# A semaphore wait that makes GpSimd follow VectorE's step at their common port

## The chip, the core and the metric

The kernel runs on one core of a Trainium2 chip. A core has five engines that run side by side, each with its own queue that it works through in order: TensorE (matmuls, PE in the profile), VectorE (DVE), ScalarE (ACT), GpSimd (POOL) and SyncE (SP, which issues most of the DMAs here). Between engines order comes from semaphores alone: an instruction waits until a counter has reached a value. The metric is device time in microseconds of one execution. Before the change it was 2434.4 us, the median of three runs (2433.55 to 2434.43).

## The reference, cut to what matters

Channel attention is followed by a feed-forward layer with a rational function between its two products.

```
qn, kn = q and k, divided by their norms over the 6080 tokens     # 4 batches, 256 channels
a = softmax(kn^T @ qn / tau)                                      # 256 x 256 for each batch
x = (v @ a), all tokens in one list                               # 24320 x 256
h = x @ w_in                                                      # 24320 x 2048
g = (a0 + a1 h + a2 h^2 + a3 h^3) / (1 + |b0||h| + |b1| h^2 + 1e-6)
out = g @ w_out                                                   # 24320 x 256
```

## The kernel before, in words

The softmax and w_in are multiplied once for each batch ("fused" weights, tile `w`), so that the long part is: values times fused weights, rational function, times w_out. Every fp32 factor is split into a high and a low part, and three products stand for one (`vhi`/`vlo`, `w` in two tiles, `gh`/`gl`, `w_high`/`w_low`).

The tokens go in groups of 512 (48 groups, 12 for each batch), and the 2048 hidden channels in 8 pairs of 128. One pair of one group, called a pair step below, is 128 x 1024 elements and passes these engines (function `pair`):

- TensorE: 12 matmuls into one of three PSUM buffers `hx`.
- ScalarE: `d` (twice: size, then square), `uu` (slope), `r` (inverse root, then its square).
- VectorE: "num" `hx<-uu,fit,hx`; "high" `gh<-hx,fit,r`; "back" `d<-d,gh`; "rest" `d<-hx,fit,d`. Rest is the last reader of `hx`, and TensorE may fill that buffer again when it is done.
- GpSimd: "low" `gl<-d,r`.
- TensorE: 8 matmuls of `gh` and 4 of `gl` into `acc`. At a group's end VectorE turns `acc` into `orow`, which is stored.

Once for each group VectorE also turns the loaded values (`cv<-vst`), ScalarE makes `vhi` of them and GpSimd the rest `vlo<-cv,vhi`. While the groups of one batch run, the q and k rows of the next batch pass through: TensorE multiplies them (`hx<-kq`), VectorE sums that into `sacc`, ScalarE squares them (`sq<-kq`, two buffers) and GpSimd sums the squares (`ssq<-sq,ssq`).

What order the instructions stand in is decided in Python before anything is built. `Planner.add` takes steps with an engine, a cost, a due time (tables `LAG` and `TIME`) and the buffers they read and write. `Planner.order` plays the steps through with these costs: on each engine the ready step with the earliest due time starts. Steps marked `port` (all GpSimd steps, back on VectorE, the transposes of values and some others on VectorE) are taken to need a port that VectorE and GpSimd share: `fits` starts such a step only when the planned port step of the other engine is over. The list that comes out has all steps in order of planned start. It fixes the order on each engine, and `InOrder` keeps it. Between engines the plan's order is not kept: an instruction waits for the data and buffers that it needs, and for nothing else. So a GpSimd step that the plan put behind a back of VectorE may start ahead of it on the chip.

The arm that runs for these inputs is `halves[True]`; it holds 515 GpSimd tensor_tensor steps: 383 `gl`, 48 `vlo` and 84 sums of squares. The last pair step is done by halves (`halved`), with its `gl` on VectorE.

Of the kernel before, what the change touches and what calls it, by code (L numbers as in the profile page):

```python
# [88 lines left out]
class InOrder:  # L89


    def __init__(self, tc, engine):
        self.tc, self.engine = tc, engine

    def __getattr__(self, name):
        op = getattr(self.engine, name)

        def issue(*args, **kwargs):
            ins = op(*args, **kwargs)  # L99
            self.tc.keep_in_program_order(ins)  # L100
            return ins

        return issue
# [14 lines left out]


class Step:  # L120
    __slots__ = ("eng", "cost", "fn", "key", "need", "after", "new", "bufs", "banks", "port", "n")


class Planner:
# [54 lines left out]
    def order(self):  # L179
# [10 lines left out]
        events, out, now = sorted((t, 2, n, None) for n, t in enumerate(busy.values())), [], 0.0  # L190
        port = {"DVE": 0.0, "POOL": 0.0}
# [18 lines left out]
        while left:  # L210
# [34 lines left out]
            while events and events[0][0] <= now:  # L245
                _, what, _, s = heapq.heappop(events)
# [7 lines left out]
                if what == 1:  # L254
                    for b in s.bufs:
                        b.left -= 1
                        if not b.left:
                            free[b.tag].append(b.slot)
        self.trace = out
        return [s for _, s in out]  # L260


@with_exitstack
def tile_channel_attention_rational_ffn(
# [58 lines left out]
    dve = InOrder(tc, nc.vector)  # L323
    act = InOrder(tc, nc.scalar)
    pool = InOrder(tc, nc.gpsimd)
# [89 lines left out]
    def near_root(x):  # L415
        act.activation(near, x, AF.Abs_reciprocal_sqrt)
# [8 lines left out]
    def fit_grow():  # L425
        dve.reciprocal(inv, b1)
        dve.tensor_tensor(left, b0, b0, op=ALU.mult)
        dve.scalar_tensor_tensor(left, left, -0.25, inv, op0=ALU.mult, op1=ALU.mult)
        dve.tensor_scalar(left, left, ONE, None, op0=ALU.add)
        dve.reciprocal(share, left)  # L430
        dve.tensor_tensor(zero, b1, share, op=ALU.mult)

    def fit_reach():
        root_of(grow, zero)
        dve.reciprocal(inv, grow)
        dve.scalar_tensor_tensor(centre, b0, 0.5, inv, op0=ALU.mult, op1=ALU.mult)
        dve.tensor_tensor(centre, centre, share, op=ALU.mult)
        dve.tensor_scalar(sign, a3, 0.0, None, op0=ALU.is_ge)
        dve.tensor_scalar(sign, sign, 2.0, 1.0, op0=ALU.mult, op1=ALU.subtract)
        dve.tensor_tensor(zero, size[:, 3:4], share, op=ALU.mult)  # L440
        for _ in range(3):
            dve.tensor_tensor(zero, zero, inv, op=ALU.mult)

    def fit_rest():
        root_of(reach, zero)
        dve.tensor_tensor(zero, reach, b1, op=ALU.mult)
        dve.reciprocal(left, zero)
        dve.tensor_tensor(shift, a2, sign, op=ALU.mult)
        dve.scalar_tensor_tensor(shift, shift, 0.5, left, op0=ALU.mult, op1=ALU.mult)
        dve.tensor_tensor(drop, a1, sign, op=ALU.mult)  # L450
        dve.tensor_tensor(drop, drop, share, op=ALU.mult)
        dve.tensor_tensor(drop, drop, inv, op=ALU.mult)
        dve.tensor_tensor(left, shift, shift, op=ALU.mult)
        dve.tensor_tensor(drop, drop, left, op=ALU.subtract)
        dve.tensor_tensor(base_a0, a0, sign, op=ALU.mult)
        dve.tensor_tensor(base_a0, base_a0, share, op=ALU.mult)

    def unscaled():
        dve.memset(fit[:, 0:2], 1.0)
        dve.tensor_copy(base_a0, a0)  # L460

    def arm(fast):
# [574 lines left out]
            finish(G, at + NFP * II + due["finish"], acc)  # L1037
        return plan.order()
    halves = {fast: arm(fast) for fast in (True, False)}
    choice = nc.values_load(plain[0:1, 0:1], min_val=0, max_val=1)  # L1040
    with tc.If(choice > 0) as which:
        fit_grow()
        near_root(zero)
        fit_reach()
        near_root(zero)
        fit_rest()
        dve.reciprocal(rtau, coef[:, 6:7])
        for s in halves[True]:
            s.fn()
    with which.Else():  # L1050
        unscaled()
        dve.reciprocal(rtau, coef[:, 6:7])
        for s in halves[False]:
            s.fn()


# [28 lines left out]
```

## Time and profile before

| what | value |
|---|---|
| median of three runs | 2434.4 us |
| the profiled execution | 2432.47 us, its span 2430.6 us |
| TensorE matmuls | 2366.0 us busy, 97% |
| VectorE | 2180.3 us busy, 90% |
| ScalarE | 2160.2 us busy, 89% |
| GpSimd | 1318.9 us busy, 54% |

The profiler takes one execution. The page gives each engine's busy time, and the chain of work that ended last (here 90% of it TensorE). The trace gives single instructions: start and length in us, engine, source line, operation, tiles written and read, shape, and in brackets the idle time before it with what ended it. All steps are recorded by one helper, so they share line 99 and are told apart by their tiles. The granted clock (PEclk) is TensorE's share of its full speed of 2.4 GHz in a stretch; half of it is the lower level of 1.2 GHz.

### The profile page before, as it was taken

Reading aid. Unit: us, or ns where it says so; the run is one execution under the profiler, and the core shown is the slowest. Engines: PE = TensorE matmul, PEld = TensorE weight load, DVE = VectorE, ACT = ScalarE, POOL = GpSimd, SP = SyncE. Lnnn points to the kernel's source line nnn. Section 1 sums busy time; section 2 is a strip of 40 time slices with the busy share of each in tenths; the row PEclk is TensorE's granted clock in tenths of the full one; section 3 lists DMA queues with packets and bytes.
Section 4 is the critical chain, followed back from the end, with each engine's and each line's share of the span. In section 5 each row is a group of like instructions: output and inputs, shape, how many; then the busy total and the mean of one; then the engine's idle time right before and its main releaser. Section 6 shows DMA issues by size and latency. Waiting matters only on the chain.

```text
span 2430.6 us, 29239 instructions
## 1 busy us (share of the span) xinstructions
PE 2366.0 (97%) x10304; PEld 1945.9 (80%) x10304; DVE 2180.3 (90%) x1959; ACT 2160.2 (89%) x2192; POOL 1318.9 (54%) x522
## 2 busy tenths in 40 slices
PE   7889999999999999999999999999999999999998
PEld 6767788888888788888888878888888788888887
DVE  8888999999977899999997789999998999999997
ACT  4678999999888799999988879999997999999996
POOL 5476555554557655554546855554554445555553
PEclk9999999999999999999999999999999999999999
DMA  9542111111124211111112411111111111111101
GB/s 294 172 114 58 25 19 27 27 26 18 27 52 131 72 22 26 27 27 17 27 27 50 133 31 27 27 24 21 26 27 18 17 27 27 19 26 27 26 9 18
DMA packets 457037, 110.04 MB, mean 45 GB/s; under 512 B 405168, under 2 KB 453808, under 8 KB 456880
## 3 DMA queue, kind: packets, MB, share of 16 engines
q1 hardware_dynamic: 454736, 107.84, 20.7%
q8 instruction: 83, 1.36, 0.2%
q14 instruction: 74, 0.61, 0.1%
q10 hardware_dynamic: 2144, 0.23, 0.1%
HBM read 83.10 MB, written 24.90 MB: 44 GB/s over the span
## 4 chain that ended last, share of the span: by engine, by line
PE 90%; DVE 4%; ACT 2%; DMA 2%; issue 1%; SPq 0%; POOL 0%; ACTq 0%; DVEq 0%; POOLq 0%
PE hx L99 49%; PE acc L99 42%; DVE d L99 2%; DVE hx L99 1%; ACT d L99 1%; DMA kq<-in_q_dram 1%; DMA d<-in_moe_w_in_dram 1%; DVE gh L99 0%; ACT r L99 0%; ACT uu L99 0%; DMA r<-in_k_dram 0%; SPq L99 0%; DVE acc L99 0%; DVE orow L99 0%; DVE fit L99 0%
## 5 line engine op out<-in xcount | busy, mean ns | idle before, releaser
L99 POOL TENSOR_TENSOR gl<-d,r 128x1024 fp32r<-128x1024 f32 (+1 forms) x383 | 955.7, 2501 | 1015.6 <-DVE d L99 660.3
L99 PE MATMUL hx<-vhi,w 128*128 128x512 f32 (+1 forms) x3072 | 901.1, 395 | 16.9 <-DVE d L99 15.2
L99 PEld LDWEIGHTS hx<-vhi,w 128*128 128x128 f32 x3072 | 579.1, 189 | 149.4 <-DVE d L99 10.7
L99 DVE SCALAR_TENSOR_TENSOR gh<-hx,fit,r 128x1024 fp32r<-128x1024 f32 (+1 forms) x385 | 484.8, 1259 | 101.3 <-ACT r L99 93.5
L99 DVE SCALAR_TENSOR_TENSOR d<-d,gh 128x1024 f32<-128x1024 f32 (+1 forms) x385 | 539.8, 1403 | 1.6
L99 DVE SCALAR_TENSOR_TENSOR hx<-uu,fit,hx 128x1024 f32<-128x1024 f32 (+1 forms) x385 | 487.6, 1267 | 57.1 <-ACT uu L99 56.5
L99 ACT ACTIVATE d<-hx 128x1024 f32<-128x1024 f32 (+1 forms) x385 | 388.6, 1010 | 130.1 <-PE hx L99 108.7
L99 DVE SCALAR_TENSOR_TENSOR d<-hx,fit,d 128x1024 f32<-128x1024 f32 (+1 forms) x383 | 483.9, 1264 | 7.0
L99 PE MATMUL acc<-gh,w_high 128*128 128x512 f32 (+1 forms) x1536 | 478.3, 392 | 4.1 <-DVE orow L99 2.7
L99 PE MATMUL hx<-vlo,w 128*128 128x512 f32 (+1 forms) x1536 | 480.0, 394 | 0.0
L99 PE MATMUL acc<-gh,w_low 128*128 128x512 f32 (+1 forms) x1536 | 475.4, 391 | 0.0
L99 ACT ACTIVATE uu<-hx,fit 128x1024 f32<-128x1024 f32 (+1 forms) x385 | 457.6, 1189 | 0.5 <-PE hx L99 0.5
L99 ACT ACTIVATE d<-d,fit 128x1024 f32<-128x1024 f32 (+1 forms) x385 | 437.4, 1136 | 0.0
L99 ACT ACTIVATE r<-d 128x1024 f32<-128x1024 f32 (+1 forms) x385 | 404.1, 1050 | 32.3 <-POOL gl L99 4.5
L99 PE MATMUL acc<-gl,w_high 128*128 128x512 f32 (+1 forms) x1536 | 408.5, 393 | 4.4 <-DVE gl L99 2.6
L99 ACT ACTIVATE r<-r 128x1024 f32<-128x1024 f32 (+1 forms) x385 | 402.1, 1044 | 4.8
L99 PEld LDWEIGHTS acc<-gl,w_high 128*128 128x128 f32 x1536 | 288.8, 188 | 68.6 <-DVE gl L99 3.0
L99 PEld LDWEIGHTS hx<-vlo,w 128*128 128x128 f32 x1536 | 291.1, 190 | 65.3
L99 PEld LDWEIGHTS acc<-gh,w_high 128*128 128x128 f32 x1536 | 288.8, 188 | 65.6 <-DVE orow L99 3.6
L99 PEld LDWEIGHTS acc<-gh,w_low 128*128 128x128 f32 x1536 | 289.2, 188 | 61.1
L99 POOL TENSOR_TENSOR ssq<-sq,ssq 128x1024 f32<-128x1024 f32 (+1 forms) x69 | 174.9, 2535 | 41.5 <-ACT sq L99 29.1
L99 POOL TENSOR_TENSOR vlo<-cv,vhi 128x1024 fp32r<-128x1024 f32 (+1 forms) x48 | 155.6, 3242 | 10.0 <-ACT vhi L99 9.5
(111 smaller groups left out, 1006.2 us busy)
## 6 DMA issues: line engine op xcount, KB each, us to landing
vst<-in_v_dram SPq DMA_DIRECT2D x352, 64.0 KB, 2.4
out_dram<-orow SPq DMA_DIRECT2D x352, 64.0 KB, 2.0
kq<-in_k_dram SPq DMA_DIRECT2D x78, 256.0 KB, 3.6
kq<-in_q_dram SPq DMA_DIRECT2D x78, 256.0 KB, 4.2
d<-in_moe_w_in_dram SPq DMA_DIRECT2D x8, 512.0 KB, 6.6
r<-in_k_dram SPq DMA_DIRECT2D x10, 256.0 KB, 6.5
r<-in_q_dram SPq DMA_DIRECT2D x10, 256.0 KB, 6.5
d<-in_moe_w_out_dram SPq DMA_DIRECT2D x4, 512.0 KB, 6.6
```

The lines of the kernel that those rows point to most:

```text
L99: ins = op(*args, **kwargs)
```

## The change

`Planner.order` walks its list once more at the end. It remembers the latest VectorE step marked `port`; the next GpSimd step of the list gets it as `behind`, and it is forgotten then, so a second GpSimd step directly after has none of its own. A function `run` issues the list, as the loop did before; it notes the last instruction of each such VectorE step, and the first GpSimd instruction of a step with `behind` gets a semaphore wait for it. VectorE gets no wait for GpSimd. Nothing else differs: the instructions of all engines, their order and their buffers are as before, and on GpSimd 33 more wait-only instructions stand in the arm that runs, since an instruction holds few waits itself. 250 of its 515 steps now wait for a later VectorE instruction than before; for the others the wait was already there through their data, or through an earlier step of the queue.

```diff
--- before.py
+++ after.py
@@ -91,6 +91,7 @@
 
     def __init__(self, tc, engine):
         self.tc, self.engine = tc, engine
+        self.last, self.behind = None, None
 
     def __getattr__(self, name):
         op = getattr(self.engine, name)
@@ -98,6 +99,11 @@
         def issue(*args, **kwargs):
             ins = op(*args, **kwargs)
             self.tc.keep_in_program_order(ins)
+            if self.behind is not None:
+                wait = mybir.DependencyInfo(mybir.DependencyClass.Sync, mybir.DependencyReason.DATA)
+                self.tc.add_manual_dep(ins.ins, self.behind, wait, reason="order at the shared port")
+                self.behind = None
+            self.last = ins.ins.name
             return ins
 
         return issue
@@ -118,7 +124,7 @@
 
 
 class Step:
-    __slots__ = ("eng", "cost", "fn", "key", "need", "after", "new", "bufs", "banks", "port", "n")
+    __slots__ = ("eng", "cost", "fn", "key", "need", "after", "new", "bufs", "banks", "port", "n", "behind", "ins")
 
 
 class Planner:
@@ -257,6 +263,13 @@
                         if not b.left:
                             free[b.tag].append(b.slot)
         self.trace = out
+        turn = None
+        for _, s in out:
+            s.behind = s.ins = None
+            if s.port and s.eng == "DVE":
+                turn = s
+            elif s.eng == "POOL":
+                s.behind, turn = turn, None
         return [s for _, s in out]
 
 
@@ -1037,6 +1050,15 @@
             finish(G, at + NFP * II + due["finish"], acc)
         return plan.order()
     halves = {fast: arm(fast) for fast in (True, False)}
+
+    def run(steps):
+        for s in steps:
+            if s.behind is not None:
+                pool.behind = s.behind.ins
+            s.fn()
+            if s.port and s.eng == "DVE":
+                s.ins = dve.last
+
     choice = nc.values_load(plain[0:1, 0:1], min_val=0, max_val=1)
     with tc.If(choice > 0) as which:
         fit_grow()
@@ -1045,13 +1067,11 @@
         near_root(zero)
         fit_rest()
         dve.reciprocal(rtau, coef[:, 6:7])
-        for s in halves[True]:
-            s.fn()
+        run(halves[True])
     with which.Else():
         unscaled()
         dve.reciprocal(rtau, coef[:, 6:7])
-        for s in halves[False]:
-            s.fn()
+        run(halves[False])
 
 
 # ---- launch: one core; inputs and outputs as the reference has them ----
```

The first place is GpSimd's queue at 806 us of the trace, in the second batch's groups. `ssq0_104` is the sum of squares, `gl0_85` and `gl1_86` the two buffers of low parts, `vlo1_109` the low part of the values; the names in brackets are the engines' semaphores. Before:

```order
L99 TENSOR_TENSOR ssq0_104<-sq1_101,ssq0_104 128x1024 [waits Activation_49,Pool_49]
L99 TENSOR_TENSOR gl1_86<-d3_75,r0_79 128x1024 [waits DVE_49,PE_49]
L99 TENSOR_TENSOR ssq0_104<-sq0_100,ssq0_104 112x1024 [waits Activation_49,Pool_49]
L99 TENSOR_TENSOR gl0_85<-d1_73,r2_81 128x1024 [waits DVE_49,PE_49]
L99 TENSOR_TENSOR ssq0_104<-sq1_101,ssq0_104 112x1024 [waits Activation_49,Pool_49]
L99 TENSOR_TENSOR vlo1_109<-cv0_112,vhi1_107 128x1024 [waits Activation_49]
L99 TENSOR_TENSOR gl1_86<-d0_72,r0_79 128x1024 [waits DVE_49,PE_49,Activation_49]
L99 TENSOR_TENSOR gl0_85<-d2_74,r1_80 128x1024 [waits PE_49,Pool_49]
```

Now:

```order
L100 TENSOR_TENSOR ssq0_104<-sq1_101,ssq0_104 128x1024 [waits Activation_49,Pool_49]
L100 TENSOR_TENSOR gl1_86<-d3_75,r0_79 128x1024 [waits DVE_49,PE_49]
L100 TENSOR_TENSOR ssq0_104<-sq0_100,ssq0_104 112x1024 [waits DVE_49,Activation_49,Pool_49]
L100 TENSOR_TENSOR gl0_85<-d1_73,r2_81 128x1024 [waits PE_49]
L100 TENSOR_TENSOR ssq0_104<-sq1_101,ssq0_104 112x1024 [waits Activation_49,Pool_49]
L100 TENSOR_TENSOR vlo1_109<-cv0_112,vhi1_107 128x1024 [waits DVE_49,Activation_49]
L100 TENSOR_TENSOR gl1_86<-d0_72,r0_79 128x1024 [waits DVE_49,PE_49,Activation_49]
L100 TENSOR_TENSOR gl0_85<-d2_74,r1_80 128x1024 [waits DVE_49,PE_49,Pool_49]
```

No step has moved. The third step, the sum of squares, now waits for VectorE, so the three behind it stand behind that wait too (`gl0_85<-d1_73,r2_81` has lost its own wait, which the earlier one covers); `vlo1_109` and the last row have a new wait each.

VectorE's queue at the same place is the same before and now. The sum of squares waits for `d2_74<-d2_74,gh2_84` (a back), `vlo1_109` for `d0_72<-d0_72,gh0_82` (the next back):

```order
L100 SCALAR_TENSOR_TENSOR gh2_84<-hx2_70,fit_166,r1_80 128x1024 [waits DVE_49,Activation_49]
L100 TENSOR_TENSOR sacc0_111<-hx0_68,sacc0_111 128x512 [waits DVE_49,PE_49]
L100 SCALAR_TENSOR_TENSOR d2_74<-d2_74,gh2_84 128x1024 [waits DVE_49]
L100 SCALAR_TENSOR_TENSOR hx1_69<-uu0_76,fit_166,hx1_69 128x1024 [waits Activation_49]
L100 SCALAR_TENSOR_TENSOR d2_74<-hx2_70,fit_166,d2_74 128x1024 [waits DVE_49]
L100 SCALAR_TENSOR_TENSOR gh0_82<-hx1_69,fit_166,r0_79 128x1024 [waits DVE_49,PE_49,Activation_49]
L100 TENSOR_TENSOR sacc0_111<-hx0_68,sacc0_111 128x512 [waits PE_49]
L100 SCALAR_TENSOR_TENSOR d0_72<-d0_72,gh0_82 128x1024 [waits DVE_49]
```

Here too nothing moved; the rest of the first back's pair step, `d2_74<-hx2_70,fit_166,d2_74`, stands two steps behind it.

The second place is GpSimd's queue from 151 to 178 us, in the first batch's groups. Before:

```order
L99 TENSOR_TENSOR ssq0_104<-sq1_101,ssq0_104 128x1024 [waits Activation_49,Pool_49]
L99 TENSOR_TENSOR ssq0_104<-sq0_100,ssq0_104 128x1024 [waits Activation_49,Pool_49]
L99 TENSOR_TENSOR gl1_86<-d2_74,r0_79 128x1024 [waits DVE_49,PE_49]
L99 TENSOR_TENSOR ssq0_104<-sq1_101,ssq0_104 128x1024 [waits Activation_49,Pool_49]
L99 TENSOR_TENSOR gl0_85<-d3_75,r1_80 128x1024 [waits DVE_49,PE_49]
L99 TENSOR_TENSOR ssq0_104<-sq0_100,ssq0_104 128x1024 [waits Activation_49,Pool_49]
L99 TENSOR_TENSOR vlo1_109<-cv0_112,vhi1_107 128x1024
L99 TENSOR_TENSOR ssq0_104<-sq1_101,ssq0_104 128x1024 [waits Activation_49,Pool_49]
L99 TENSOR_TENSOR gl1_86<-d1_73,r2_81 128x1024 [waits PE_49]
```

Now:

```order
L100 TENSOR_TENSOR ssq0_104<-sq1_101,ssq0_104 128x1024 [waits DVE_49,Activation_49,Pool_49]
L100 TENSOR_TENSOR ssq0_104<-sq0_100,ssq0_104 128x1024 [waits DVE_49,Activation_49,Pool_49]
L100 TENSOR_TENSOR gl1_86<-d2_74,r0_79 128x1024 [waits PE_49]
L100 TENSOR_TENSOR ssq0_104<-sq1_101,ssq0_104 128x1024 [waits Activation_49,Pool_49]
L100 TENSOR_TENSOR gl0_85<-d3_75,r1_80 128x1024 [waits DVE_49,PE_49]
L100 TENSOR_TENSOR ssq0_104<-sq0_100,ssq0_104 128x1024 [waits DVE_49,Activation_49,Pool_49]
L100 TENSOR_TENSOR vlo1_109<-cv0_112,vhi1_107 128x1024
L100 TENSOR_TENSOR ssq0_104<-sq1_101,ssq0_104 128x1024 [waits Activation_49,Pool_49]
L100 TENSOR_TENSOR gl1_86<-d1_73,r2_81 128x1024 [waits PE_49]
```

The second row waits for the back of `d3_75`, with the two rows behind it in its wake; the sixth, a sum of squares, waits for the next back, of `d0_72`, and the `vlo1_109` behind it with it.

## Rows read from the trace of the kernel before

**Rows 1.** The page, busy us, share of the span, instructions

```profile
PE 2366.0 (97%) x10304; PEld 1945.9 (80%) x10304; DVE 2180.3 (90%) x1959; ACT 2160.2 (89%) x2192; POOL 1318.9 (54%) x522
```

**Rows 2.** Waits of TensorE: us in total, times, longest us

```profile
PE hx L99 <- DVE d L99: 22.4, 9, 4.3
...
PE acc L99 <- POOL gl L99: 1.8, 2, 1.0
```

**Rows 3.** Windows: stretch, its us, busy by engine, PEclk, DMA share, GB/s

```profile
850.00:1265.00 415.00, 415.00 (x1822) 340.89 (x1821) 390.56 (x332) 391.47 (x386) 216.33 (x84) 1.00 0.15 24
```

**Rows 4.** Timeline of VectorE around 815 us: start us, us, instruction [idle before]

```profile
812.78 7.14 DVE L99 SCALAR_TENSOR_TENSOR d<-d,gh 128x1024 f32<-128x1024 f32 x1
...
821.04 1.27 DVE L99 SCALAR_TENSOR_TENSOR d<-hx,fit,d 128x1024 f32<-128x1024 f32 x1
...
824.02 1.21 DVE L99 SCALAR_TENSOR_TENSOR d<-d,gh 128x1024 f32<-128x1024 f32 x1
```

**Rows 5.** Timeline of GpSimd around 815 us

```profile
811.78 2.41 POOL L99 TENSOR_TENSOR ssq<-sq,ssq 112x1024 f32<-112x1024 f32 x1 [1.02 <-ACT sq L99]
814.15 2.38 POOL L99 TENSOR_TENSOR gl<-d,r 128x1024 fp32r<-128x1024 f32 x1
816.49 2.35 POOL L99 TENSOR_TENSOR ssq<-sq,ssq 112x1024 f32<-112x1024 f32 x1
```

**Rows 6.** Timeline of TensorE, the two idle times of 4.11 us

```profile
822.46 1.19 PE L99 MATMUL hx<-vhi,w 128*128 128x512 f32 x2 [4.11 <-DVE d L99]
...
1414.28 1.06 PE L99 MATMUL hx<-vhi,w 128*128 128x512 f32 x2 [4.11 <-DVE d L99]
```

**Rows 7.** Windows behind these two idle times, and one at full clock

```profile
822.40:828.10 5.70, 5.64 (x15) 4.48 (x16) 2.83 (x3) 0.35 (x1) 0.00 (x0) 0.57 0.00 1
828.10:834.00 5.90, 5.90 (x27) 4.80 (x26) 2.58 (x3) 5.90 (x7) 0.61 (x1) 1.00 0.00 0
1414.20:1419.90 5.70, 5.62 (x18) 4.50 (x19) 2.85 (x3) 1.01 (x2) 0.00 (x0) 0.70 0.00 0
```

**Rows 8.** Timeline of VectorE and GpSimd, 151 to 172 us

```profile
151.88 2.48 DVE L99 SCALAR_TENSOR_TENSOR gh<-hx,fit,r 128x1024 fp32r<-128x1024 f32 x2 [1.54 <-ACT r L99]
154.27 6.03 DVE L99 SCALAR_TENSOR_TENSOR d<-d,gh 128x1024 f32<-128x1024 f32 x2
160.22 2.46 DVE L99 SCALAR_TENSOR_TENSOR d<-hx,fit,d 128x1024 f32<-128x1024 f32 x2
...
155.87 3.35 POOL L99 TENSOR_TENSOR gl<-d,r 128x1024 fp32r<-128x1024 f32 x1
```

**Rows 9.** Timeline of TensorE, 161 us, and the window behind it

```profile
161.55 8.86 PE L99 MATMUL hx<-kq 128*128 128x256 f32 x32 [4.33 <-DVE d L99]
...
161.50:170.50 9.00, 8.95 (x34) 7.59 (x35) 4.32 (x5) 1.06 (x1) 8.69 (x5) 0.81 0.37 115
```

**Rows 10.** Timeline of VectorE around 200 us

```profile
198.26 2.73 DVE L99 SCALAR_TENSOR_TENSOR d<-d,gh 128x1024 f32<-128x1024 f32 x1
```

**Rows 11.** Timeline of TensorE around 203 us

```profile
202.21 0.84 PE L99 MATMUL acc<-gh,w_high 128*128 128x512 f32 x2 [2.70 <-DVE orow L99]
202.84 1.05 PE L99 MATMUL acc<-gh,w_low 128*128 128x512 f32 x2
```

**Rows 12.** Timeline of TensorE around 688 us

```profile
687.56 8.90 PE L99 MATMUL hx<-w_in_sb,eT 128*128 128x256 f32 x40 [0.58 <-DVE d L99]
```

**Rows 13.** Timeline of VectorE in the last pair

```profile
2416.63 1.19 DVE L99 SCALAR_TENSOR_TENSOR d<-d,gh 128x448 f32<-128x448 f32 x1
```

**Rows 14.** Timeline of VectorE and GpSimd at 443 us, in a steady stretch

```profile
443.39 1.21 DVE L99 SCALAR_TENSOR_TENSOR d<-d,gh 128x1024 f32<-128x1024 f32 x1
...
443.64 3.23 POOL L99 TENSOR_TENSOR gl<-d,r 128x1024 fp32r<-128x1024 f32 x1 [3.64 <-DVE d L99]
```

**Rows 15.** Timeline of GpSimd and TensorE, a vlo and its first reader

```profile
167.45 2.37 POOL L99 TENSOR_TENSOR vlo<-cv,vhi 128x1024 fp32r<-128x1024 f32 x1
...
178.77 0.62 PE L99 MATMUL hx<-vlo,w 128*128 128x512 f32 x2
```


## The prediction

> **What bounds the kernel now.** I read the page first: TensorE's matmuls are busy for 2366.0 of 2430.6 us [rows 1], so some 65 us are all that can be won on its idle time, and a further part where its clock is low. Then windows: in the long stretches between the batches' fronts TensorE is busy for 415.00 of 415.00 us at a clock of 1.00 [rows 3]. A change to VectorE or GpSimd wins or loses nothing there unless it makes TensorE wait. So I asked for TensorE's waits. The largest entry is 22.4 us in nine waits for VectorE's step on `d` [rows 2]: the rest step, which reads `hx` last and gives the buffer back. GpSimd's `gl` makes it wait for 1.8 us only.
>
> Last came timelines around these waits. At 812.78 us a back on VectorE takes 7.14 us; the next one takes 1.21 [rows 4]. GpSimd had begun a sum of squares at 811.78, and ran a `gl` and a second sum directly behind it, to 818.84 (816.49 + 2.35) [rows 5]. VectorE's step ends at 819.92, 1.08 after that. A GpSimd step that is under way holds VectorE's back, and steps that follow without a gap hold it all along. The other way round it is the same: at 443.64 us a `gl` begins 0.25 us into a back and takes 3.23 us [rows 14], against some 2.4 for steps that meet none [rows 5].
>
> The change decides who goes first. Where GpSimd ran ahead of the plan, VectorE now passes it; where VectorE was first already, GpSimd waits at a semaphore rather than at the port.
>
> **Two places of 4.11 us.** TensorE is idle for 4.11 us before 822.46, and again before 1414.28 [rows 6], where the same steps meet in the next batch. It wants the `hx` buffer that the rest at 821.04 gives back at 822.31 [rows 4]. By the change the sum of squares waits for the back. The back starts at 812.78 as before, since it waits for nothing new, and takes 1.21 us; all of VectorE's work behind it moves forward by 7.14 - 1.21 = 5.93 us, so the rest ends at 816.4. TensorE is done with its work before at 822.46 - 4.11 = 818.35, so the wait goes altogether: 4.11 us at each place, 8.2 in all.
>
> The clock comes on top. Behind the first idle time the granted clock is 0.57 of full speed for 5.7 us, mostly the lower level of 1.2 GHz, and behind the second 0.70 [rows 7]. In 5.7 us 15 matmuls ran where at full clock 27 take 5.9; 15 would have taken 3.3 us, so 2.4 us were lost. Behind the second it is 18 matmuls, 3.9 us, 1.8 lost. Without the idle time I count the clock as full: 4.2 us. If the chip lowers it all the same, that is nothing. The place is worth 8.2 to 12.4 us; I take 12.4, as the clock was 1.00 up to the idle time.
>
> **The first batch's stretch.** From 154.27 two backs take 6.03 us together, while GpSimd's queue runs into them; the `gl` at 155.87 also grows to 3.35 us [rows 8]. Both backs at 1.21 would end at 156.7, the first rest behind them (2.46 for two) at 157.95, and TensorE would start its q and k products there and not at 161.55 [rows 9]: 3.55 us. They can't come earlier: the highs at 151.88 wait for ScalarE [rows 8], which the port doesn't touch. An idle time of 4.33 - 3.55 = 0.8 us is left. The clock was 0.81 for 9.0 us behind it [rows 9], which is 1.7 us; I count that as won in half.
>
> At 198.26 a back takes 2.73 us [rows 10], and the transpose that empties `acc` stands behind it; TensorE waits for that transpose for 2.70 us, to 202.21, and its next pairs of matmuls take 1.05 us against 0.62 elsewhere [rows 11, 15]. Without the hold VectorE is ready 1.52 us earlier, at 199.5, when TensorE is done too (202.21 - 2.70); some 1.35 of the wait goes, the transpose itself stays. Five pairs at the low rate lose 5 x (1.05 - 0.62) = 2.1 us at most; half of it is 1. This stretch is worth 4.9 to 8.7; I take 3.55 + 0.85 + 1.35 + 1 = 6.75.
>
> **Small ones.** TensorE waits 0.58 us at 687.56 for a rest that stands behind a held back [rows 12], and as long once more a batch later: 1.2 us. In the last pair a back of half size takes 1.19 us [rows 13] where half of 1.21 is to be expected; the low behind it is what TensorE waits for at the end: 0.55 us. The four other waits for `d`, 22.4 - 4.33 - 2 x 4.11 - 2 x 0.58 = 8.7 us, stay: at two of them the GpSimd step that holds the back stands ahead of it in the plan too, and at the two before 150 us the chain of ScalarE is as late.
>
> **What it costs.** A GpSimd step that the port would have held now starts after the semaphore. At 443 us the back ends at 444.60 and the `gl` at 446.87, 2.27 us later [rows 14]. A semaphore's way took 0.15 us from VectorE's rest, ended at 822.31, to TensorE's start at 822.46 [rows 4, 6]; I take it for GpSimd too, with bounds of 0 and 0.3. With a whole step of 2.4 that is 2.4 to 2.7: 0.1 to 0.4 us later each time, for one `gl` and one `vlo` in each group. A `gl` that is 0.3 us late is hidden by the two `gl` buffers, since TensorE waited for GpSimd but twice [rows 2]. Extra wait instructions are 33 in all, on an engine that is idle for 46% of the span; I put them at nothing.
>
> Where GpSimd was ahead it is held for longer, and everything queued behind it. At 811.78 the first sum starts after 814.0, 2.3 us later, and the `gl`, the second sum and the `vlo` behind it too. Its squares buffers are wanted again by ScalarE long after. In the first stretch it is tighter: the sum at 165.14 has to wait for a back at 171.06 that itself comes some 3.5 to 5 us earlier than before, and the `vlo` behind it, begun at 167.45, ends 2.5 to 4 us later than its 169.82. Its first reader on TensorE started at 178.77 [rows 15] and moves to 174 or 175. Between them 1 to 2 us are left: hidden, but that is the thinnest cover.
>
> **A rule weighed.** The Trainium skill ("SBUF — State Buffer", section "SBUF: two separate sides") says that whichever of the two instructions starts first has the shared pair for that whole instruction, and the other blocks. By that alone a waiting back would be let in at the end of the sum under way, at 814.19, end at 815.4, and TensorE would not have waited at 822; the two large places would be worth nothing and the sum 20.4 - 12.4 = 8.0 us. The trace shows that the back waited through three steps of GpSimd's queue, to 818.84 [rows 4, 5], so the measurement decides.
>
> **The sum.** 12.4 + 6.75 + 1.75 = 20.9 us, less 0 to 1 us of new waits for GpSimd, say 0.5: 20.4. The profiled execution took 2432.47 us, 1.9 below the median of the runs; I take the difference over to the median: 2434.4 - 20.4 = 2414.
>
> **Rivals.**
> - *Half of it comes back a step later* (2424 us). At the two large places TensorE goes on at 818.35 and wants another `hx` buffer after 36 matmuls (two products and 12 into `acc`), at 0.22 us each [rows 7] about 826.3. The rest that gives it up stands behind the num of the first of these products, so after its 12 matmuls, two steps of ScalarE of about 1.2 and two of VectorE: 818.35 + 2.7 + 2.4 + 2.5 = 825.9. If that chain is later by 2.4 us, some 2 us of idle time stand there in place of 4.11 and the clock falls as before: 2 x (2 + 2) = 8 less, and 10 if the clock of the first stretch is not won either. For it speaks that the margin is 0.4 us; against it, that both ends of it move with TensorE's own start, and the clock is back at 1.00 from 828.1 on in the trace [rows 7], so that nothing was missed there before.
> - *Nothing that TensorE sees* (2431 to 2437). VectorE is set free but waits for ScalarE's `r` or `uu` instead, so that the rest comes as late. Then 0 to 3 us are won and the small costs stand against them. Against it: the rest at 821.04 begins 1.12 us after the held back's end at 819.92 [rows 4], one step's time, so neither it nor the step between had to wait for anything else.
> - *GpSimd becomes the late engine* (slower, 2446). Place: the fronts' stretches, where its queue is nearly without gaps (8.69 of 9.0 us at 161.5 [rows 9]). Each is held back twice by about 3.8 us at steps that had run ahead. If a `gl` or `vlo` behind them comes later than TensorE's need, TensorE waits; it decides at the first reader of `vlo`, where I count 1 to 2 us of cover. If VectorE's gain came to nothing in two of the three stretches and one hold of 3.8 us reached TensorE in each, it would be 3 x 3.8 = 11.4 us more, 2446.
>
> **How the numbers follow.** The forecast (2407 to 2420) has 0.60, the half 0.20, nothing 0.13, slower 0.07. A difference of 0.2%, 4.9 us, is about what a measurement can tell from no change, so faster means below 2429.5: the first two and a little of the third, 0.81; same 0.12; slower 0.07. The upper bounds of the terms (12.4 + 8.7 + 1.75, and 4 us, half of the waits that I count as staying) lead to 2407; the lower ones (8.2 + 4.9 + 1) to 2420. The range goes from 2405 to 2429, which holds the first two cases. The likeliest case's own range is 2407 to 2420.
>
> **What would show it.** In the new profile TensorE's waits for `d` fall from 22.4 to about 9 us, and the idle times before 822 and 1414 are gone with the low clock behind them. No back takes 7 us; the mean of the 1024-wide ones falls below 1.35 us. `vlo` takes about 2.4 us and no longer 3.3. It would be wrong if backs still took 3 us and more in these stretches (the port isn't what held them), or if TensorE's waits for `gl` or `vlo` grew by as much as those for `d` fall.

## The result, and the profile after

The changed kernel takes 2406.9 us (median of four runs, 2405.45 to 2408.11), the kernel before 2434.0 on the same chip (2429.33 to 2434.43): a ratio of 0.9891, with a 95% interval of 0.9879 to 0.9902. That is 27.0 us less, where 20.4 were forecast. The profiled executions took 2432.47 and 2408.11 us, so 24.4 us are there to be found in the two traces.

The page of the changed kernel (busy us, share of the span, instructions) answers to [rows 1]:

```profile
PE 2358.0 (98%) x10304; PEld 1939.0 (81%) x10304; DVE 2155.4 (90%) x1959; ACT 2162.3 (90%) x2192; POOL 1229.4 (51%) x522
```

TensorE's matmuls are busy for 8.0 us less with the same number of instructions: that is clock (0.993 of full speed in the mean, 0.988 before). The other 16 us are idle time. GpSimd's 89.5 us and VectorE's 24.9 us less I read as time in which one of them stood at the port; most of it never reached TensorE. The waits of TensorE (total us, times, longest) answer to [rows 2]:

```profile
PE hx L100 <- DVE d L100: 8.8, 5, 2.4
PE acc L100 <- POOL gl L100: 1.8, 2, 1.0
PE acc L100 <- DVE orow L100: 1.3, 1, 1.3
```

The waits for `d` have gone from 22.4 us to 8.8, those for GpSimd's `gl` are the same 1.8 in two waits, and the 2.70 us for the transpose at 202.21 [rows 11] are 1.3 (at 194.84 now).

The first of the two large places, 815 us before, stands at 803 us now. VectorE and GpSimd there (start, us), for [rows 4, 5]:

```profile
802.57 1.22 DVE L100 SCALAR_TENSOR_TENSOR d<-d,gh 128x1024 f32<-128x1024 f32 x1
803.71 1.28 DVE L100 SCALAR_TENSOR_TENSOR hx<-uu,fit,hx 128x1024 f32<-128x1024 f32 x1
804.90 1.28 DVE L100 SCALAR_TENSOR_TENSOR d<-hx,fit,d 128x1024 f32<-128x1024 f32 x1
...
809.33 2.79 DVE L100 SCALAR_TENSOR_TENSOR d<-d,gh 128x1024 f32<-128x1024 f32 x1
```

```profile
803.96 2.38 POOL L100 TENSOR_TENSOR ssq<-sq,ssq 112x1024 f32<-112x1024 f32 x1 [2.09 <-DVE d L100]
806.30 2.38 POOL L100 TENSOR_TENSOR gl<-d,r 128x1024 fp32r<-128x1024 f32 x1
808.63 2.40 POOL L100 TENSOR_TENSOR ssq<-sq,ssq 112x1024 f32<-112x1024 f32 x1
812.26 2.41 POOL L100 TENSOR_TENSOR vlo<-cv,vhi 128x1024 fp32r<-128x1024 f32 x1 [1.23 <-DVE d L100]
```

The back takes 1.22 us in place of 7.14, and the rest that gives `hx` back ends at 806.2, 3.6 us after the back's start, as forecast (812.78 to 816.4). The sum of squares starts 0.17 us after the back's end; GpSimd was idle for 2.09 us before it. TensorE's work behind both places, for [rows 6, 7], in windows (columns as in [rows 3]):

```profile
807.70:813.40 5.70, 5.70 (x27) 4.65 (x26) 4.73 (x4) 2.46 (x3) 4.47 (x3) 1.00 0.58 182
1391.40:1397.10 5.70, 5.70 (x26) 4.65 (x26) 4.72 (x4) 2.47 (x3) 4.47 (x3) 1.00 0.00 0
```

The idle times of 4.11 us are gone, and the clock is 1.00 where it was 0.57 and 0.70: 27 and 26 matmuls in 5.7 us in place of 15 and 18. The next back meets the second sum, which the plan has ahead of it, and takes 2.79 us.

The first batch's stretch, for [rows 8, 9, 15]: VectorE's two backs, TensorE's q and k products with the idle time before them, GpSimd's `vlo` and its first reader, and the window from 157 us.

```profile
153.61 2.35 DVE L100 SCALAR_TENSOR_TENSOR d<-d,gh 128x1024 f32<-128x1024 f32 x2
```

```profile
157.22 7.17 PE L100 MATMUL hx<-kq 128*128 128x256 f32 x32 [0.71 <-DVE d L100]
...
172.75 0.62 PE L100 MATMUL hx<-vlo,w 128*128 128x512 f32 x2
```

```profile
166.76 2.37 POOL L100 TENSOR_TENSOR ssq<-sq,ssq 128x1024 f32<-128x1024 f32 x1 [1.25 <-DVE d L100]
169.08 2.41 POOL L100 TENSOR_TENSOR vlo<-cv,vhi 128x1024 fp32r<-128x1024 f32 x1
```

```profile
157.00:166.00 9.00, 8.78 (x40) 7.66 (x41) 6.10 (x7) 4.31 (x5) 8.51 (x4) 1.00 0.67 195
```

Both backs take 2.35 us together in place of 6.03, the idle time of 4.33 is 0.71, and the clock behind it is 1.00 where it was 0.81. One back of this stretch is 2 us longer than before: the one at 198.50 takes 3.34 us (1.23 before, at 205.74), as a sum that the plan has ahead of it had started 0.16 us earlier. The prediction names backs of 3 us and more in these stretches as a sign of being wrong; this is the only one there, and TensorE has no wait for `d` behind it that it did not have before. The cover of `vlo` has shrunk as forecast: it ends at 171.49 and is read at 172.75, 1.26 us later.

Groups by form (instruction, count, then busy us and mean ns of one):

```profile
L100 DVE SCALAR_TENSOR_TENSOR d<-d,gh 128x1024 f32<-128x1024 f32 x352 | 476.7, 1355 | 1.4
L100 POOL TENSOR_TENSOR vlo<-cv,vhi 128x1024 fp32r<-128x1024 f32 x44 | 106.2, 2415 | 57.5 <-DVE d L100 52.6 <-ACT vhi L100 3.6 <-ACT r L100 1.2
```

`vlo` takes 2.4 us, as forecast. The back's mean is 1355 ns, 5 ns above the bound I had set for it.

### The profile page after: what moved, and what is told of

Same layout as the page of the kernel before. It is cut to its first block, busy times and chain, and to the rows that moved or that the text cites. A ratio compares the mean times of both kernels' runs of the same rounds, so it can differ in the third digit from the quotient of the medians.

```text
span 2406.2 us, 29272 instructions
## 1 busy us (share of the span) xinstructions
PE 2358.0 (98%) x10304; PEld 1939.0 (81%) x10304; DVE 2155.4 (90%) x1959; ACT 2162.3 (90%) x2192; POOL 1229.4 (51%) x522
## 4 chain that ended last, share of the span: by engine, by line
PE 93%; DVE 2%; DMA 2%; ACT 2%; issue 1%; SPq 0%; POOL 0%; ACTq 0%; DVEq 0%; POOLq 0%
PE hx L100 50%; PE acc L100 43%; ACT d L100 1%; DMA d<-in_moe_w_in_dram 1%; DMA kq<-in_q_dram 1%; DMA kq<-in_k_dram 0%; ACT r L100 0%; DVE hx L100 0%; DVE gh L100 0%; DVE d L100 0%; SPq L100 0%; DMA r<-in_k_dram 0%; ACT uu L100 0%; DVE acc L100 0%; DVE orow L100 0%
## 5 line engine op out<-in xcount | busy, mean ns | idle before, releaser
L100 POOL TENSOR_TENSOR gl<-d,r 128x1024 fp32r<-128x1024 f32 (+1 forms) x383 | 914.5, 2394 | 1004.8 <-DVE d L100 693.2
L100 DVE SCALAR_TENSOR_TENSOR d<-d,gh 128x1024 f32<-128x1024 f32 (+1 forms) x385 | 515.1, 1338 | 1.6
L100 POOL TENSOR_TENSOR ssq<-sq,ssq 128x1024 f32<-128x1024 f32 (+1 forms) x69 | 165.8, 2404 | 68.7 <-DVE d L100 20.5
L100 PE MATMUL hx<-kq 128*128 128x256 f32 (+1 forms) x592 | 138.1, 388 | 15.8 <-DVE fit L100 7.0
```

## The experiments

All times are medians, set against runs of the kernel before on the same chip (2431.5 to 2433.4 in the three groups of runs). The first five kernels have part of the waits: `run` of the changed kernel with another condition.

**Only the sums of squares wait.**

```diff
-            if s.behind is not None:
+            if s.behind is not None and any(b.tag == "sq" for b in s.bufs):
```

> The added waits stay at GpSimd's sums of squares alone (ssq, orow); its gl and vlo steps have none. Theory: TensorE's time was lost where a sum of squares had run ahead of a held back, in the three stretches in which the next batch's q and k pass. So nearly all of the gain stays: 22 to 26 us below the kernel before, of some 27; what goes is the last pair's 0.5 us and a little at vlo. Rival (many small collisions: one gl and one vlo in each of 48 groups no longer start into a back): most of the gain is in the waits left out, and this kernel is 5 to 12 us below the kernel before.

Measured: 2407.8 us, ratio 0.9894 (0.9879 to 0.9909), 25.6 us less. The waits at the sums give what the whole change gives. `vlo` is back at 3261 ns in this kernel (mean), and that costs nothing that the median shows.

**Only `gl` and `vlo` wait.** The same line with `not any(...)`.

> The other half: the added waits at gl and vlo alone, none at the sums of squares. Theory: 0 to 3 us below the kernel before, most of it the last pair's 0.5 us; vlo takes 2.4 us as in the changed kernel, and TensorE does not see it. Rival (many small collisions): 15 to 22 us below.

Measured: 2423.3 us, 0.9964 (0.9951 to 0.9978), 10.1 less: the theory with 0 to 3 is wrong, and so is the rival with 15 to 22. VectorE's back at the first place, and GpSimd there:

```profile
816.49 4.83 DVE L100 SCALAR_TENSOR_TENSOR d<-d,gh 128x1024 f32<-128x1024 f32 x1
```

```profile
815.49 2.41 POOL L100 TENSOR_TENSOR ssq<-sq,ssq 112x1024 f32<-112x1024 f32 x1 [1.10 <-ACT sq L100]
817.85 2.39 POOL L100 TENSOR_TENSOR gl<-d,r 128x1024 fp32r<-128x1024 f32 x1
820.18 3.35 POOL L100 TENSOR_TENSOR ssq<-sq,ssq 112x1024 f32<-112x1024 f32 x1
```

None of these three steps waits for this back, and they follow each other without a gap. Yet the back got in, at the end of the `gl`: it ends at 821.32, 1.08 us after 820.24, and the second sum, blocked by it, takes 3.35 us. So GpSimd's steps without a gap do not hold the port all along, as I had written. My own rows had shown it: the `gl` of 3.35 us at 155.87 [rows 8] is one that let a back in ahead of it.

**Two waits alone**, at the two sums of 811.78 and 1403.60 us:

```diff
+        turns = [s for s in steps if s.eng == "POOL"]
+        held = {id(turns[i]) for i in (183, 314)}
...
+            if s.behind is not None and id(s) in held:
```

> Two waits only of the 250: at the two sums of squares that start at 811.78 and at 1403.60 us in the trace of before, each for the back that follows it there. Theory: both idle times of 4.11 us go with the low clock behind them, 8.2 + 2.4 + 1.8 = 12.4 us below the kernel before, at least 10. Rival (the gain needs the whole order, or the idle time only moves on to the next buffer): 0 to 5 us.

Measured: 2419.7 us, 0.9949 (0.9935 to 0.9962), 13.7 less, against 12.4 forecast for this term. Two of the waits make half of the gain.

**The wait one step later**, at the `gl` behind each of these two sums: `held = {id(turns[i + 1]): turns[i].behind for i in (183, 314)}`.

> The same two waits, one GpSimd step later: the sum of squares runs ahead as before, and the gl behind it waits for the back. Theory (VectorE's back is kept out as long as GpSimd's steps follow each other without a gap, and gets in at the first gap): the back starts to move at the sum's end, 814.2, ends at 815.4, the rest at 817.8, ahead of TensorE's need at 818.35; so the gain is that of two waits at the sums, 10 to 12.4 us, and the back takes about 2.7 us instead of 7.14. Rival (who starts first decides, and VectorE must pass the sum itself to win): 0 to 4 us.

Measured: 2418.1 us, 0.9940 (0.9926 to 0.9953), 15.3 less. VectorE's back, and GpSimd:

```profile
814.62 2.49 DVE L100 SCALAR_TENSOR_TENSOR d<-d,gh 128x1024 f32<-128x1024 f32 x1
```

```profile
813.61 2.42 POOL L100 TENSOR_TENSOR ssq<-sq,ssq 112x1024 f32<-112x1024 f32 x1 [1.05 <-ACT sq L100]
817.26 2.38 POOL L100 TENSOR_TENSOR gl<-d,r 128x1024 fp32r<-128x1024 f32 x1 [1.23 <-DVE d L100]
```

Held by one sum alone the back takes 2.49 us, and TensorE doesn't feel it. The loss before was that three steps held it, not that one did.

**The first stretch alone**: `held = {id(s) for s in turns[:59]}`.

> The changed kernel with the waits at the first 59 GpSimd steps alone, which are those of the stretch up to some 205 us; all later steps start as in the kernel before. Theory (the first stretch is a gain of its own, which nothing later takes back): 8 to 9 us less than before, all of it there by 205 us, as TensorE's instructions came 8.6 us earlier there in the changed kernel; the two idle times of 4.11 us near 815 and 1407 us remain, with the low clock behind them. Rival (TensorE gets the time back as a wait at the next front, where the rows of q and k are loaded at their own pace): 0 to 4 us less. The three runs with parts of the change then account for the whole: two places 13.7 us, first stretch 8 to 9, and 3 to 5 of small ones.

Measured: 2423.0 us, 0.9965 (0.9952 to 0.9979), 9.3 less, a little above the 8 to 9 of the theory; in its trace TensorE is 7.9 us ahead of before at 205 us. TensorE's idle times in its trace are those of the changed kernel at the first two rows and that of the kernel before at the third:

```profile
157.91 7.17 PE L100 MATMUL hx<-kq 128*128 128x256 f32 x32 [0.71 <-DVE d L100]
...
195.54 0.74 PE L100 MATMUL acc<-gh,w_high 128*128 128x512 f32 x2 [1.34 <-DVE orow L100]
...
814.16 1.17 PE L100 MATMUL hx<-vhi,w 128*128 128x512 f32 x2 [4.11 <-DVE d L100]
```

With the two waits this makes 13.7 + 9.3 = 23.0 of the 27.0 us.

The next four ask why a back took 7.14 us, if VectorE is let in at the end of a GpSimd step. Six sums of squares have 112 rows (the last token group of a batch): the two at each of the large places, and two in the first batch, at 195.15 and 199.86 us. All other GpSimd steps have 128. These kernels are the one before, with no new wait, and change the rows of one line:

```diff
-                    fn = lambda: e.tensor_tensor(total[:pn], sq[:pn], total[:pn], op=ALU.add)
+                    rows = pn if own else P
+                    fn = lambda: e.tensor_tensor(total[:rows], sq[:rows], total[:rows], op=ALU.add)
```

**All sums over 128 rows** (the diff above).

> The kernel before, without any of the new waits; only GpSimd's sums of squares of each batch's last token group go over all 128 rows in place of 112 (the rows 112 to 127 then add squares left over from an earlier group, so the norms differ from the reference's). A step takes as long as before. Theory (VectorE's held back is let in at the end of a GpSimd step, also between two that follow without a gap; only behind a step of 112 rows is it not, as a part of GpSimd has nothing to do in it and begins the next step early): the backs at 812.8 and 1404.6 us take 2.5 to 3.5 us and no longer 7.14, the low part that follows the sum grows from 2.4 to about 3.3, both idle times of TensorE of 4.11 us go, and the run is 10 to 13 us faster than before. Rival (steps that follow each other without a gap hold the port all along, whatever their rows; what I wrote in the prediction): both backs still take 7.1 us, and the time is the same within 2 us.

Measured: 2418.7 us, 0.9947 (0.9933 to 0.9961), 13.5 less: as much as the two waits gave, without a wait. VectorE, then GpSimd:

```profile
813.26 2.48 DVE L99 SCALAR_TENSOR_TENSOR d<-d,gh 128x1024 f32<-128x1024 f32 x1
```

```profile
812.25 2.41 POOL L99 TENSOR_TENSOR ssq<-sq,ssq 128x1024 f32<-128x1024 f32 x1 [1.04 <-ACT sq L99]
814.62 3.35 POOL L99 TENSOR_TENSOR gl<-d,r 128x1024 fp32r<-128x1024 f32 x1
```

The back gets in between the sum and the `gl`, which grows to 3.35 us, just as the theory said.

**All sums over 112 rows**: `rows = pn if own else 112`.

> The opposite of the run with full rows: the kernel before, without the new waits, with all of GpSimd's sums of squares over 112 rows (the squares of the rows 112 to 127 are left out of the norms). A step takes as long as before. Theory (behind a step of 112 rows GpSimd doesn't let a waiting back in): in the stretches in which GpSimd's queue is nearly full (120 to 200, 760 to 815, 1350 to 1405 us) several more backs take 4.8 us and more, TensorE's waits for the step on d rise from 22.4 us to 40 or more, and the run is 10 to 40 us slower than before. Rival (rows don't matter): no back is longer than in the kernel before, and the time is the same within 2 us.

Measured: 2433.6 us, 1.0008 (0.9999 to 1.0017). The theory said 10 to 40 us slower: wrong. Both backs of 7.14 us are there, but no third. VectorE and GpSimd at a sum of 112 rows that now lets a back in, and VectorE at the old place:

```profile
804.02 2.20 DVE L99 SCALAR_TENSOR_TENSOR d<-d,gh 128x1024 f32<-128x1024 f32 x1
...
815.02 7.14 DVE L99 SCALAR_TENSOR_TENSOR d<-d,gh 128x1024 f32<-128x1024 f32 x1
```

```profile
802.64 2.40 POOL L99 TENSOR_TENSOR ssq<-sq,ssq 112x1024 f32<-112x1024 f32 x1 [1.15 <-ACT sq L99]
805.01 3.45 POOL L99 TENSOR_TENSOR gl<-d,r 128x1024 fp32r<-128x1024 f32 x1
```

So in these runs 112 rows are needed for the long hold, but not enough.

**The first sum of each pair full, the second short** (`rows = P if half == 0 and not own else pn`), and **the other way round** (`half == 1`).

> The kernel before, without new waits, with the first of the two sums of 112 rows of a batch over all 128 rows (811.78 us), the second as before (the rows 112 to 127 of an older square are added, so the norms differ). Theory (the part that runs ahead does so from the first short step on): the back gets in at the end of the first sum, in 2.5 us, TensorE's idle times of 4.11 us go, 10 to 13 us faster than before. Rival (both short steps are needed, or the second alone does it): the back takes 4.8 us or 7.14, and the gain is 0 to 8 us.

> As the run with the first sum full, with the second sum of the two (816.49 us) full and the first as before. Theory of the part that runs ahead: it begins the gl during the short sum, the second sum during the gl and the vlo during the second sum, so the back is held to the end of the second sum or longer: 7.14 us or more, and no gain beyond 2 us. Rival (only the end of a short step, or the end of a step before a short one, is closed to VectorE): the back gets in at the end of the gl, in 4.8 us, TensorE's idle times shrink to 1.5 to 2 us, and the run is 6 to 8 us faster.

Measured: with the first sum full 2421.2 us, 0.9958 (0.9941 to 0.9974), 10.3 less; the back takes 2.49 us. With the second full and the first short 2439.6 us, 1.0037 (1.0023 to 1.0051): 8.2 us slower than the kernel before. Its back, its GpSimd and its TensorE at the first place:

```profile
818.60 9.44 DVE L99 SCALAR_TENSOR_TENSOR d<-d,gh 128x1024 f32<-128x1024 f32 x1
```

```profile
817.60 2.42 POOL L99 TENSOR_TENSOR ssq<-sq,ssq 112x1024 f32<-112x1024 f32 x1 [1.05 <-ACT sq L99]
819.96 2.38 POOL L99 TENSOR_TENSOR gl<-d,r 128x1024 fp32r<-128x1024 f32 x1
822.30 2.36 POOL L99 TENSOR_TENSOR ssq<-sq,ssq 128x1024 f32<-128x1024 f32 x1
824.62 2.34 POOL L99 TENSOR_TENSOR vlo<-cv,vhi 128x1024 fp32r<-128x1024 f32 x1
```

```profile
830.57 1.19 PE L99 MATMUL hx<-vhi,w 128*128 128x512 f32 x2 [6.41 <-DVE d L99]
```

One short step at the head, and the back waits through four steps, to the end of the `vlo` at 826.96 (it ends 1.08 us later). The idle time at 830.57 grows from 4.11 to 6.41 us. In the first batch the back of 2.73 us [rows 10] takes 5.04 here, and TensorE waits 5.00 us for the transpose behind it.

**Two waits at the `vlo` behind the second sum alone**: `held = {id(turns[i]) for i in (186, 317)}` in the changed kernel.

> The changed kernel with the waits at two GpSimd steps alone: the vlo behind the second of the two sums of 112 rows, in both batches (818.80 us in the kernel before). Both sums and the gl between them start as before. Theory (a part of GpSimd that has nothing to do in a step of 112 rows runs ahead into the vlo and so holds the port over one more boundary; a vlo that is held can't be run ahead into): the back at 812.8 takes 4.8 us in place of 7.14, as in the run with the waits at gl and vlo alone, TensorE's two idle times shrink from 4.11 to 1.5 to 2 us, and the run is 6 to 8 us faster than before. Rival (that the back got in earlier in that run came from its other waits): 7.14 us again, and the same time as before within 2 us.

Measured: 2426.8 us, 0.9979 (0.9969 to 0.9988), 4.7 less, a bit under the 6 to 8 expected. The back takes 4.82 us, as said, and TensorE is idle for 1.79 us at each place: 2 x (4.11 - 1.79) = 4.6 us. The median fits the idle time alone. The trace also has the gain in clock that I had added; behind the first place:

```profile
819.80:825.50 5.70, 5.68 (x25) 4.64 (x26) 3.27 (x4) 2.63 (x3) 2.40 (x1) 1.00 0.26 85
```

This execution is the fastest of the ten (2422.66 us, 8.8 below the median of before, mean clock 0.993); the other nine ran at 0.988 to 0.991. Where they lost it I can't say, as one execution was traced.

**What a late GpSimd costs**: one `vlo` computed twice, another three times.

```diff
+        again = {id(turns[38]): 1, id(turns[186]): 2}
...
+            for _ in range(again.get(id(s), 0)):
+                s.fn()
```

> The changed kernel with one vlo step computed twice (the one at 169.08 us, in the first stretch) and another three times (the one at 812.26 us); the result is the same. It prices the rival that GpSimd becomes the late engine. In the changed kernel the first vlo ends at 171.49 and TensorE reads it at 172.75; the second ends at 814.67 and is read at 816.74. Theory (the cover is 1.26 and 2.07 us, and what goes beyond it is TensorE's idle time): TensorE waits 1.2 to 1.4 us at the first and 2.8 to 3.0 at the second, and the run is 4 to 6 us slower than the changed kernel, that is 21 to 23 us faster than before, the clock behind the second included. Rival (TensorE's later waits take it up, or the buffers give more cover than these times show): 0 to 2 us slower than the changed kernel.

Measured: 2415.7 us (2410.41 to 2416.37), 0.9932 (0.9918 to 0.9945) of before; against the changed kernel's 0.9891 that is some 10 us slower, twice what was expected. The profiled execution is the fastest of the five, only 2.3 us above the changed kernel's; the other four ran at a mean clock of 0.990 to 0.991 against its 0.993, and I have no trace of them. In its trace TensorE loses 1.4 us at the first place and 2.9 at the second against the changed kernel, 4.3 together and so within the 4 to 6 expected; up to the first place it had been 1.1 us ahead. What the other four lost beyond that is not shown. TensorE, ScalarE, TensorE in its trace:

```profile
172.91 0.73 PE L100 MATMUL hx<-vlo,w 128*128 128x512 f32 x2 [1.08 <-POOL vlo L100]
```

```profile
822.91 1.06 ACT L100 ACTIVATE r<-d 128x1024 f32<-128x1024 f32 x1 [3.14 <-POOL gl L100]
```

```profile
830.84 0.74 PE L100 MATMUL hx<-vhi,w 128*128 128x512 f32 x2 [2.62 <-DVE d L100]
```

The first wait is about the one expected: 2.4 us more work, less the cover of 1.26, 1.08 us of idle time. At the second place I had the wrong reader. TensorE does not wait for that `vlo`; the `gl` behind it is late, ScalarE waits for the `r` buffer that this `gl` reads (in the changed kernel it ended 0.87 us ahead of ScalarE's need), and the rest comes late in its wake. `gl` is covered less well by `r` than by its own two buffers.

## Why the prediction was right, and where it was not

The direction and the places were right, because the terms were read from idle times that the change did remove. The size was short: 27.0 us against 20.4, and 2406.9 lies just below the likeliest case's own range (2407 to 2420). The two profiled executions differ by only 24.4 us, as that of before was 1.5 us faster than its median and that of the changed kernel 1.2 slower; these 2.7 us no trace can place. Where the changed kernel's TensorE stands against before, instruction by instruction, gives each term from the two profiled traces:

| term | forecast, us | measured, us |
|---|---|---|
| first stretch to 205 us | 6.75 | 8.6 (that stretch alone: 9.3 in the median, 7.9 in its trace at 205 us) |
| two large places, idle time | 8.2 | 8.9 |
| their clock | 4.2 | 3.6 (both parts in the kernel with two waits: 12.5 in its trace, 13.7 in the median) |
| small ones | 1.75 | about 3 |
| new waits for GpSimd | -0.5 | none seen in TensorE's waits |

- *First stretch.* The mis-sized term. I had counted half of the clock behind 161.55 and 202.84 as won; all of it came. TensorE's lead grew by 1.7 us from 161.5 to 165 (0.85 counted) and by 1.2 from 202 to 205 (1.0 counted). The two idle times gave 3.6 and 1.4, as forecast (3.55 and 1.35). The other 0.7 us TensorE had won by 155 us: it was 0.85 us late at 130 and gained 1.55 by a higher clock behind 131 us (last section). The kernel with the waits of this stretch alone has nothing of it at 155 us, so I put it down to chance.
- *Two large places.* Right in size, and by the runs with two waits it is these two steps that do it. The rival that half of it comes back a step later did not happen: no idle time stands behind either place.
- *Small ones.* The two waits of 0.58 us are gone, and the last wait for VectorE's `gl` fell from 2.6 to 2.04 us, as forecast in both. The other waits for `d` stayed: 8.8 us where I had said about 9.
- *GpSimd late.* The cover at the first `vlo` was what I had said, and the run with more work on GpSimd shows that TensorE pays as soon as it is gone. I missed the second cover, ScalarE's `r`.
- *The step that was wrong* is "steps that follow without a gap hold it all along", and with it the verdict on the rule of the Trainium skill ("SBUF — State Buffer", "SBUF: two separate sides"). That rule, the port is held for one instruction at a time, is what the runs show wherever steps have 128 rows: with full sums the back of 7.14 us takes 2.48. It fails behind a short first step: 7.14 and 9.44 us. The forecast of the two places didn't hang on why the back waited, only on its 7.14 us, so the error cost nothing in the sum. It would have cost in any other change: by my reading full rows would have won nothing, and they win 13.5 us.

What a short step does can be read so: a part of GpSimd has no rows in it, goes on to the next step while the others work, and so the port is in use at the moment at which they change steps. Three runs speak for it: a full first sum opens the port (2.49 us), a full second one keeps it closed for longer (9.44), and a `vlo` that is held back opens it one step earlier (4.82). Beside it, the Trainium skill ("GPSIMD Engine Reference", "2.1 Instruction dispatch") says that each of GpSimd's cores serves 16 partitions of every instruction and starts the next one as soon as its own share is done; rows 112 to 127 are one core's share. That this core is the cause is inferred, not shown.

A short sum alone does not do it, as the one at 802.64 in the kernel with short sums shows. What sets the two kinds apart in the traces is when the buffer of the `gl` behind the sum comes free, which is when TensorE has read it to the end. In that kernel:

```profile
798.71 1.07 PE L99 MATMUL acc<-gl,w_high 128*128 128x512 f32 x4
...
814.02 1.27 PE L99 MATMUL acc<-gl,w_high 128*128 128x512 f32 x4
```

Ahead of the sum at 802.64 the last reading had ended at 799.78; that of 814.02 ended at 815.29, 1.3 us into the sum at 814.01. In all the traces together a back stood waiting at the end of a short sum with a `gl` directly behind it 19 times. It was kept out 13 times, and each time the reading ended during the sum; it got in 6 times, all in the kernel with short sums, and each time the reading had ended before the sum began. This fits the reading above: the part without rows begins a `gl` whose buffer is there together with the sum, and ends with it; one whose buffer comes free later it begins later, and is in the middle of it when the others change steps. No run moved that moment by itself, so this too is inferred.

## What to carry to other kernels

Where two engines share a port, look for the few places at which one of them is held for longer than a single step of the other: here two of 250 waits made half the gain, and most of the 89.5 + 24.9 us of busy time that went from GpSimd and VectorE was never on the path. Price a wait by where it ends on the engine that bounds, its clock included, and count the cover of every buffer that the held engine gives back, not only of what it writes. A step that leaves part of GpSimd's rows out takes as long as a full one and can shut VectorE out through several steps; try full rows before adding waits, with zeros in the added rows (the run here added old squares, so its norms were others than the reference's).

## What the runs showed of the hardware that was not expected

A low clock does not stand behind every idle time of a given length. In both kernels TensorE is idle for 2.42 us at about 130 us, before the same matmuls. The kernel before, TensorE and the window behind (columns as in [rows 3]):

```profile
131.06 1.22 PE L99 MATMUL hx<-vhi,w 128*128 128x512 f32 x2 [2.42 <-DVE d L99]
```

```profile
131.00:136.70 5.70, 5.64 (x18) 4.53 (x19) 5.70 (x8) 5.24 (x6) 3.56 (x2) 0.70 0.42 127
```

The changed kernel:

```profile
131.91 0.73 PE L100 MATMUL hx<-vhi,w 128*128 128x512 f32 x2 [2.42 <-DVE d L100]
```

```profile
131.90:137.60 5.70, 5.69 (x25) 4.55 (x26) 5.70 (x7) 5.70 (x7) 3.54 (x2) 1.00 0.41 133
```

The first pair of matmuls takes 1.22 us before and 0.73 now, and the clock behind is 0.70 against 1.00, though the idle time and the matmuls behind it are the same. The change alone does not make the difference. The kernel with the waits of the first stretch alone has the same instructions and waits as the changed one up to there, and the same idle time of 2.42 us before 131.08, and its clock is as low as before:

```profile
131.00:136.70 5.70, 5.62 (x18) 4.45 (x19) 5.70 (x7) 5.23 (x6) 3.54 (x2) 0.70 0.42 136
```

I have no explanation that a run has tested. It is one reason why clock terms of a forecast are safer given as a range.

A sum of squares of 112 rows takes 2.41 us on GpSimd at 811.78 [rows 5] and one of 128 rows 2.41 at 812.25 in the kernel with full rows: rows left out save no time.
